# The four weight sums of the first z1 group, recorded seven z2 groups earlier on GpSimd

## The chip, the cores and the metric

The kernel runs on one core of one Trainium2 chip. The metric is the device time of one execution in microseconds; the figure for a kernel is the median of its runs. A core has five engines with a queue in order each: TensorE (PE, with its weight loads shown as PEld), VectorE (DVE), ScalarE (ACT), GpSimd (POOL) and SyncE (SP), which issues DMAs.

## The reference

The input `x` has 2048 rows of 1024. A first block adds to it a memory-augmented attention over the normalised rows (32 heads, four segments of 512). The second block, a gated MLP, is the part that matters here; cut to its core it is

```python
z  = gelu(layernorm(h) @ w_in)              # w_in: 1024 x 3584
z1 = z[..., :1792]
z2 = layernorm(z[..., 1792:])
g  = einsum('ts,bsf->btf', w_sp, z2) + b_sp[None, :, None]
h2 = h + (z1 * g) @ w_out                   # w_sp: 2048 x 2048, w_out: 1792 x 1024
```

All inputs and the output are bf16.

## The kernel before

The program is written with a recorder: every call `pe.matmul(...)`, `pool.tensor_tensor(...)` and so on is appended to the list of its engine, with the waits that follow from the memory it reads and writes. Each engine then works through its own list in order. **The order in which calls are recorded is thus the order of each engine's queue**; every instruction is issued from one helper line (L210 in the profile), so the profile is read by tile names.

The stages that touch the change:

* **z2 groups.** `z2_group(k, tc)` computes 128 rows (`tc`, 0 to 15) by 448 columns (`k`, 0 to 3) of the second half of `z`: eight matmuls of 128x448, then a gelu on ACT into `z`. The list `todo` gives their order. After each group `z2_stats` records `bn_stats` on DVE (`zst`); when `k` is 3 it also records the aggregate on DVE (`zmv`), and two tiny instructions on POOL that turn the variance into a reciprocal deviation (`zrs`, an add and a power).
* **The `aux` table.** `at(q, f, ...)` puts a small job beside a z2 group: group `(k, tc)` runs the jobs of `q = 16 k + tc - 20`, after its matmuls and gelu and before its statistics. So q = 29 is group (3, 1) and q = 36 is group (3, 8). In this table stand the squares of the `w_sp` rows (ACT, `sj`), the scaling of the z1 weights to f16 (`wz_half`, DVE, q = 26 to 33, tile `wzh`; the first tile's two halves are q = 26 and 27), half-sized differences of the normalised rows (`hn_sum`, DVE, tile `ht`; q = 28, 30, 32 and 34 for the second half of the rows), a cast on POOL at q = 37 (`sqb`), and the four weight sums of the first z1 group (`sz_sum(0, k)`, POOL, tile `sz`).
* **z1 steps.** The first half of `z` is computed transposed by a seven-product scheme in the manner of Strassen. There are 14 groups `g`; each has seven steps `z1_step(g, k)` of four matmuls of 128x512 on PE. Step 1, 2 and 4 use weights `wzh` as they are; steps 5, 6, 7 and 3 use the sums 1, 2, 3 and 4 of the group's weights, which `sz_sum` forms on POOL, one TENSOR_TENSOR of 128x512 f16 each. Sum 2 is made from sum 1, and sum 4 from sum 2. Sums 1 to 3 have one buffer each, shared by all groups; sum 4 has two in turn. The sums of group `g + 1` are recorded inside the steps of group `g`: sums 1 and 2 with step 5, sum 3 with step 7; sum 4 comes two groups ahead. For the first group there is no earlier one, so its sums stand in `aux`. Sum 4 of group 1 is recorded with step 2 of group 0.
* **Order of steps.** `offs = {1: -5, 6: 0, 5: 1, 7: 3, 2: 4, 4: 6, 3: 12}` is added to `7 g` and sorted. The first steps are therefore (0,1), (0,6), (0,5), (1,1), (0,7), (0,2), (0,4), (1,6), (1,5), (2,1), (1,7), where (g,k) is group and step. Later groups have one more step, (g-1,3), between (g,2) and (g,4).
* During z1 the scaled `z2h` is written too: on DVE (with step 6) and on ACT (with step 4, after a small POOL instruction `znm`).

After z1 come two gate stages with the product by `w_sp` (again seven products per group) and the product by `w_out`; the change touches none of them.

Of the kernel before, what the change touches and what calls it, by code (L numbers as in the profile page):

```python
# [258 lines left out]
def bass_sequential_preLN__memory_aug_infini_attn__mixer_gmlp__prompt_kernel(  # L259
# [734 lines left out]
    def at(q, f, *a):  # L994
        aux.setdefault(q, []).append((f, a))
# [18 lines left out]
    for k in range(4):  # L1014
        at(28 + 2 * k, hn_sum, 1, 1 + k // 2, k % 2)
    for k in (1, 2, 3, 4):
        at(35 + k, sz_sum, 0, k)

    todo = [(0, 2), (0, 3), (0, 8), (0, 9), 0, (0, 10), 1, (0, 11), 2, (1, 0), 3]
    todo += [(1, tc) for tc in range(1, 4)] + [(0, tc) for tc in range(12, NTC)]  # L1020
# [513 lines left out]
```

## Time and profile before

| | before |
|---|---|
| runs, us | 754.74, 755.83, 756.22 |
| median, us | 755.83 |
| profiled execution: span, us | 753.7 |
| profiled execution: own time beside the span | not given apart from the span |
| PE busy | 748.3 us (99%), 5470 matmuls |
| DVE busy | 557.1 us (74%) |
| ACT busy | 421.6 us (56%) |
| POOL busy | 296.3 us (39%) |
| chain that ended last | PE 90%, DMA 3%, ACT 3%, DVE 2%, POOL 2% |

The span runs from the first to the last instruction of one execution; times in the trace are counted from its start. In a timeline, a line is a start, a length and what ran, with the number of like instructions merged into it (x4); a bracket tells the idle time before it and what ended it. Matmuls overlap, so the length of a merged block is longer than the distance to the next one. The z2 groups of `k` = 3 lie at about 380 to 404 us, the z1 steps from 404.74 us on.

### The profile page before, as it was taken

The numbers are of one execution on the slowest core, as the hardware profiler recorded it, in microseconds if no ns is written. First come the engines' busy times: TensorE is split into PE (matmuls) and PEld (weight loads), VectorE is DVE, ScalarE is ACT, GpSimd is POOL, SyncE is SP. The second block draws the span as 40 slices with busy tenths as digits, with TensorE's granted clock in tenths as the row PEclk, the third lists the DMA queues.
The fourth block names the chain that finished last, engine by engine and source line by source line (L and its number), as shares of the span: only waits on it lengthen the run. The fifth ranks groups of instructions, "written<-read, shape, count | busy, mean of one in ns | idle before, by whom it ended". The sixth has DMA issues, their size and how long they took to land.

```text
span 753.7 us, 13510 instructions
## 1 busy us (share of the span) xinstructions
PE 748.3 (99%) x5470; PEld 359.1 (48%) x5470; DVE 557.1 (74%) x1013; ACT 421.6 (56%) x519; POOL 296.3 (39%) x450
## 2 busy tenths in 40 slices
PE   9999999999999999999999999999999999999998
PEld 4445455555554445545554444444444444444444
DVE  5585589768975576677986796997885385989776
ACT  6777877787777767325894879733231355300000
POOL 2565456555654334010039988622220011222342
PEclk9999999999999999999999999999999999999999
DMA  9554546444523331678650027330019961001211
GB/s 304 171 164 83 96 75 134 99 72 93 120 58 84 119 79 43 162 188 254 192 169 0 1 41 142 56 98 1 0 21 142 262 198 35 0 1 41 79 50 57
DMA packets 136783, 75.09 MB, mean 100 GB/s; under 512 B 98064, under 2 KB 126480, under 8 KB 136720
## 3 DMA queue, kind: packets, MB, share of 16 engines
q1 hardware_dynamic: 129184, 67.14, 37.0%
q10 hardware_dynamic: 7536, 7.08, 3.5%
q8 instruction: 43, 0.70, 0.4%
q14 instruction: 20, 0.16, 0.1%
HBM read 42.74 MB, written 8.39 MB: 68 GB/s over the span
## 4 chain that ended last, share of the span: by engine, by line
PE 90%; DMA 3%; ACT 3%; DVE 2%; POOL 2%; issue 0%; ACTq 0%; DVEq 0%
PE ps L210 90%; DMA sj<-in_B_w_sp_dram 2%; ACT sj L210 2%; POOL zrs L210 1%; DMA wv<-in_A_wv_dram 1%; POOL sz L210 1%; DVE zst L210 1%; ACT z L210 1%; DVE wzh L210 1%; DVE ht L210 0%; DVE zmv L210 0%; ACT L210 0%; DVE fin L210 0%; ACTq L210 0%; DVE top L210 0%
## 5 line engine op out<-in xcount | busy, mean ns | idle before, releaser
L210 ACT ACTIVATE e<-ps 128x2048 bf16<-128x2048 f32 (+1 forms) x96 | 152.6, 1590 | 41.7 <-PE ps L210 41.5
L210 POOL TENSOR_SCALAR_AFFINE_SELECT e<-e 128x512 bf16<-128x512 bf16 x128 | 90.9, 723 | 131.2 <-ACT e L210 131.2
L210 PE MATMUL ps<-win,hnT 128*128 128x448 bf16 x512 | 98.4, 352 | 0.0
L210 POOL TENSOR_TENSOR tmp_s1b<-tmp_s,brow 128x512 f32<-128x512 f32 x28 | 36.4, 1301 | 121.6 <-DVE tmp_u L210 63.0
L210 PEld LDWEIGHTS ps<-win,hnT 128*128 128x128 bf16 x512 | 49.6, 98 | 46.3 <-issue 0.2
L210 PE MATMUL ps<-xnT,wk 128*128 128x512 bf16 x256 | 60.8, 380 | 0.0
L210 DVE TENSOR_TENSOR zt<-ps,zt 128x512 f32<-128x512 f32 x70 | 48.2, 689 | 16.8 <-PE ps L210 13.5
L210 PE MATMUL ps<-xnT,wq 128*128 128x512 bf16 x256 | 60.5, 379 | 0.0
L210 PE MATMUL ps<-wv,xnT 128*128 128x512 bf16 x256 | 60.0, 381 | 0.3 <-DMA wv<-in_A_wv_dram 0.2
L210 PE MATMUL ps<-wo,oT 128*128 128x512 bf16 x256 | 58.0, 379 | 0.0
L210 ACT ACTIVATE z<-ps 128x448 bf16<-128x448 f32 x60 | 30.4, 545 | 33.4 <-PE ps L210 33.4
L210 PE MATMUL ps<-w_out,z1T 128*128 128x512 bf16 x224 | 48.6, 379 | 0.0
L210 DVE BATCH_NORM_STATS2 zst<-z 128x6 f32<-128x448 bf16 x64 | 37.9, 611 | 10.3 <-ACT z L210 10.2
L210 PEld LDWEIGHTS ps<-v,e 128*128 128x128 bf16 x1280 | 38.8, 96 | 14.0 <-issue 6.5
L210 DVE RECIPROCAL rd<-ps 128x16 f32<-128x16 f32 x32 | 8.0, 250 | 47.0 <-PE ps L210 46.8
L210 PE MATMUL ps<-v,e 128*128 128x33 bf16 x1280 | 42.2, 178 | 0.0
L210 ACT ACTIVATE tmp_s<-ps,invy 128x512 f32<-128x512 f32 x7 | 4.8, 688 | 63.3 <-POOL tmp_s1b L210 35.9
L210 POOL TENSOR_TENSOR sz<-wzh 128x512 f16<-128x512 f16 x28 | 34.5, 1232 | 8.3 <-PE ps L210 8.3
L210 PEld LDWEIGHTS ps<-wo,oT 128*128 128x128 bf16 x256 | 24.1, 98 | 27.5
L210 PEld LDWEIGHTS ps<-xnT,wk 128*128 128x128 bf16 x256 | 22.6, 98 | 29.9 <-issue 5.0
L210 ACT ACTIVATE z1T<-zt,inv 128x512 bf16<-128x512 f32 x42 | 29.0, 715 | 13.1 <-DVE zt L210 13.1
L210 PEld LDWEIGHTS ps<-wv,xnT 128*128 128x128 bf16 x256 | 23.1, 98 | 27.3 <-DMA wv<-in_A_wv_dram 0.9
(204 smaller groups left out, 1459.8 us busy)
## 6 DMA issues: line engine op xcount, KB each, us to landing
sj<-in_B_w_sp_dram SPq DMA_DIRECT2D x16, 512.0 KB, 3.7
xch<-in_A_x_dram SPq DMA_DIRECT2D x16, 256.0 KB, 3.7
xr<-in_A_x_dram SPq DMA_DIRECT2D x16, 256.0 KB, 4.0
out_dram<-hch SPq DMA_DIRECT2D x16, 256.0 KB, 2.4
win<-in_B_w_in_dram SPq DMA_DIRECT2D x4, 896.0 KB, 5.3
wz<-in_B_w_in_dram SPq DMA_DIRECT2D x6, 512.0 KB, 8.0
wo<-in_A_wo_dram SPq DMA_DIRECT2D x1, 2048.0 KB, 8.4
fin<-out_dram ACTq DMA_DIRECT2D x16, 128.0 KB, 3.1
```

The lines of the kernel that those rows point to most:

```text
L210: ins = getattr(e, op.name)(*op.args, **op.kw)
```

## The change

One number: the four sums of the first z1 group move from q = 36 to 39, z2 groups (3, 8) to (3, 11), to q = 29 to 32, groups (3, 1) to (3, 4). The instructions stay the same. In POOL's list each of them now stands ahead of seven `zrs` pairs that it stood behind; at q = 29 its jobs in `aux` stand behind the `wz_half` of that q, which is on another engine.

```diff
     for k in range(4):
         at(28 + 2 * k, hn_sum, 1, 1 + k // 2, k % 2)
     for k in (1, 2, 3, 4):
-        at(35 + k, sz_sum, 0, k)
+        at(28 + k, sz_sum, 0, k)
```

## The prediction, on record before the result

> **What bounds the kernel now.** I read the page first: TensorE (PE) is busy 748.3 of the 753.7 us, and 90% of the chain that ended last is PE work at a granted clock of 9 tenths or more in every slice. A change on another engine can therefore give only what PE spends waiting for that engine. So next came the waits, for 380 to 430 us, around the seam between the z2 groups and the z1 steps.
>
> ```profile
> PEld ps L210 <- POOL sz L210: 1.5, 1, 1.5
> PE ps L210 <- POOL sz L210: 1.0, 1, 1.0
> ```
>
> Columns: who waited for whom, total us, times, longest. GpSimd (POOL), writing a weight sum `sz`, holds PE up once; over the whole span PE's other waits are 1.2 and 0.2 us long and lie at the start. The PE timeline (start, length, instructions) shows where:
>
> ```profile
> 409.05 1.03 PE L210 MATMUL ps<-hnT,wzh 128*128 128x512 bf16 x4
> 410.00 1.04 PE L210 MATMUL ps<-z1x,wzh 128*128 128x512 f16 x4
> 412.06 1.90 PE L210 MATMUL ps<-z1x,sz 128*128 128x512 f16 x8 [1.02 <-POOL sz L210]
> ...
> 416.42 1.03 PE L210 MATMUL ps<-hnT,sz 128*128 128x512 bf16 x4
> 417.28 1.03 PE L210 MATMUL ps<-z1x,wzh 128*128 128x512 f16 x4
> ```
>
> Ends overlap, so I count starts. Undisturbed, a block of four takes 0.86 us (416.42 to 417.28). The block of 410.00 is step (0,4) of the first z1 group; the next, step (1,6), is due at 410.86 and starts at 412.06: **1.20 us lost**. It reads sum 2 of group 1. The chain in order of time says why that sum is late:
>
> ```profile
> 395.70 0.23 POOL zrs L210
> ...
> 397.40 1.12 POOL sz L210
> ...
> 403.41 1.12 POOL sz L210
> ...
> 409.64 1.13 POOL sz L210
> 410.78 0.07 issue
> 410.85 1.17 POOL sz L210
> 412.02 0.05 issue
> 412.06 338.53 PE ps L210 x1578
> ```
>
> From 395.70 to 412.02 the chain is POOL without a gap: the small `zrs` pairs of the z2 row statistics, the four sums of group 0 (the first at 397.40, the last at 403.41), more `zrs`, then sums 1 and 2 of group 1. POOL is a queue in order, and it runs behind. After 412.06 the chain is PE alone for 338.53 us.
>
> **The change, step by step.** Nothing is added or removed: four POOL TENSOR_TENSOR of 128x512 f16 (1.15 us each in their rows at 397 to 404) move ahead of seven `zrs` pairs each, the last three also ahead of a `sqb` CAST of 0.2 us. No DMA moves, and no queue but POOL's changes. The question is only whether POOL had room earlier.
>
> ```profile
> 374.31 0.20 POOL L210 CAST sqb<-sqz 128x14 bf16<-128x14 f32 x1 [43.37 <-DVE sqz L210]
> 387.93 0.58 POOL L210 TENSOR_SCALAR zrs<-zmv 128x1 f32<-128x1 f32 x1 [13.42 <-DVE zmv L210]
> 388.60 0.87 POOL L210 TENSOR_TENSOR zrs<-zrs,mhz 128x1 f32<-128x1 f32 x1
> 389.96 0.58 POOL L210 TENSOR_SCALAR zrs<-zmv 128x1 f32<-128x1 f32 x1 [0.50 <-DVE zmv L210]
> ```
>
> It had: 13.42 us idle before 387.93, then gaps of 0.50, 0.20, 0.50, 0.20 and 0.19 (1.59 us) up to 395.70.
> 1. The first sum needs the two halves of the first scaled weight tile; the second half, a VectorE (DVE) `wzh` of 0.73 us at 383.29, ends at 384.02. In the new order this sum stands ahead of the `zrs` pair of 387.93, so it runs at about 384.1 to 385.3, wholly in idle time: POOL's backlog loses 1.15.
> 2. The other three follow the first three `zrs` pairs and fill the 1.59 us of gaps. The last `zrs`, which ends now where the next sum starts (409.61), ends at 409.61 - 1.15 - 1.59 = 406.87 by POOL's work. Its input, the last `zmv` of DVE (406.17 + 0.26 = 406.43), allows 406.43 + 0.82 (a pair, 408.79 to 409.61) = 407.25. The later one holds: 407.25.
> 3. Sum 1 of group 1 overwrites what PE reads in the pair of blocks from 405.60 to 407.49. In later groups the sum follows such a pair by 0.09 us, so it can start at 407.58. **The backlog is no longer last; PE's own read is.**
> 4. Sums 1 and 2 together take 2.40 us now (409.61 to 412.01) and 3.01 where DVE works beside them (432.21 to 435.22). So sum 2 is seen by PE, 0.05 later, at 410.03 to 410.64. The weight load that needs it is due 0.21 us ahead of its matmul (417.93 for 418.14), at 410.65. Both ends are in time: the wait goes whole.
>
> What is late next: at (0,4) the load waits 0.41 for DVE, which still reads the bank; that follows PE and stays (0.09 by starts, so the gain is at most 1.29). Sum 1 of group 2 is freed by PE and has a full period of 6.05 us, as later groups, which show no such wait. Sums 3 and 4 of group 1 are read by the steps at 413.45 and later and are ready at about 411.1 and 412.2. Nothing behind 412 us waits on a clock of its own by the PE waits, so 1.20 should reach the end.
>
> **What could cost.** The sums move beside other DVE work. These rows, DVE and then POOL, bound it:
>
> ```profile
> 385.14 0.68 DVE L210 TENSOR_TENSOR ht<-hnT,hnT 128x1024 f16<-128x1024 bf16 x1
> ...
> 398.42 0.57 DVE L210 BATCH_NORM_STATS2 zst<-z 128x6 f32<-128x448 bf16 x1
> ...
> 432.55 1.64 DVE L210 TENSOR_TENSOR ht<-hnT 128x1024 f16<-128x1024 bf16 x1
> ```
>
> ```profile
> 432.21 1.44 POOL L210 TENSOR_TENSOR sz<-wzh 128x512 f16<-128x512 f16 x1 [0.88 <-PE ps L210]
> 433.73 1.49 POOL L210 TENSOR_TENSOR sz<-sz,wzh 128x512 f16<-128x512 f16 x1
> ```
>
> Beside statistics a sum takes 1.15 and disturbs nothing (0.57 at 398.42). Beside an `ht` subtraction both suffer: DVE 1.64 for 0.68 (+0.96), POOL 1.49 for 1.15 (+0.34). The new place has four `ht` (385.14 to 394.16) and DVE busy 7.53 of 7.70 us from 388.0. Low end: nothing. High end, POOL: three sums at +0.34 make 406.87 into 407.89, sum 2 is seen at 410.34 to 410.95, and up to 0.30 of the wait stays. High end, DVE: four times 0.96 is 3.84; DVE idles 2.01 of the 9.00 us from 395.70 and another 0.89 before 406.73, so its last `zmv` is 0.94 late, sum 2 is seen 0.62 later than in step 4, at 410.65 to 411.26, and up to 0.61 stays. PE itself reads none of this DVE work before 404.7. I take the low end, because the sums fall at about 384.1, 389.5, 392.0 and 394.4 (each pair and sum taking 2.5), where at most three can meet an `ht`: 2.88 of DVE delay, just inside its 2.01 + 0.89 = 2.90 of slack. The gain is 1.20, bounds 0.59 to 1.29.
>
> [...]
>
> **The sum.** The page gives no time of its own for the profiled execution beside the span of 753.7; the three runs (754.74 to 756.22) lie 1.0 to 2.5 above it, the median 2.13. 753.7 - 1.20 = 752.5 of span, and 752.5 + 2.13 = **754.63 us**, 0.16% less. What a measurement of this kernel can tell from no change is about 0.2%, 1.51 us, so I forecast a true gain that is just under that line.
>
> **Rivals.**
> - *Part of the wait stays* (bounds above): gain 0.59 to 0.9, 754.9 to 755.2. For it: the `ht` rows. Against: DVE's idle time after 395.70.
> - *Nothing changes*, because sum 2 is held by PE's read of its buffer and not by the backlog: 755.8. Against: sum 2's buffer is last read by the step of 405.60, long before 410.85, and POOL has no idle time before it.
> - *The wait is longer outside the profile.* If the runs stall as the load row says (1.51) or more, 754.3 or below. The profile can't exclude it.
> - *Slower: DVE is blocked for a whole sum each time.* Place: 384 to 396 us. Price: four times 1.49 = 5.96 of DVE delay, less 2.90 of slack: the last `zmv` comes 3.06 later, at 409.49, its `zrs` ends at 410.31, and sum 2 at 412.71 to 413.32 instead of 412.01. That is 0.7 to 1.3 slower, 756.5 to 757.1; it turns into a loss from a DVE delay of 4.7 to 5.3. Against: no row shows more than 0.96, and the statistics, half of DVE's work there, show none.
>
> **Chances.** Forecast 0.66, part stays 0.12, longer wait 0.10, no effect 0.07, slower 0.05. The runs before lie 1.48 apart, so a comparison may read 0.7 to either side; 1.51 is 0.31 from the forecast, and I give four in ten of its cases to "faster". Faster by over 0.2%: 0.4 x 0.66 + 0.10 + 0.02 = 0.38. Slower by over 0.2%: less than the slower rival's 0.05, as its price is mostly below 1.51: 0.04 with scatter. Within: 0.58. The range takes the forecast with 1.0 below it, and reaches above to the no-effect case with 0.4 of scatter: 753.6 to 756.2. It leaves out most of the slower rival.
>
> **What would show it.** Right: in the profile after, the first sum runs near 384.1 in what was idle time; POOL waits for DVE or PE again before 409; sum 1 of group 1 starts near 407.6; no PE wait for `sz` remains; blocks at 410.00 and 410.86; PE's chain from the seam to the end is as long as before. Wrong: a PE wait for `sz` or for DVE near 410, `ht` rows of 1.64 at 385 to 395 that push the last `zmv` beyond 406.6, or a new PE wait later that takes the 1.20 back.

## The result, and the profile after

| | before | after |
|---|---|---|
| median of 19 runs, us | 755.64 | 754.43 |
| lowest to highest, us | 754.74 to 756.22 | 753.47 to 755.12 |
| span of the profiled execution, us | 753.7 | 752.2 |
| chain that ended last | PE 90% | PE 98% |

The ratio is 0.9983, 95% interval 0.9977 to 0.9990: 1.21 us, where 1.20 was forecast. Measured again on another chip (11 runs) the changed kernel had 754.55 against 755.53, ratio 0.9988, interval 0.9979 to 0.9997. The gain is small; both intervals lie below 1, and both hold the forecast ratio of 0.9984 (754.63 to 755.83).

The PE timeline of the kernel after, at the seam (start, length, instructions):

```profile
409.65 1.04 PE L210 MATMUL ps<-z1x,wzh 128*128 128x512 f16 x4
410.56 1.90 PE L210 MATMUL ps<-z1x,sz 128*128 128x512 f16 x8
```

From step (0,4) to step (1,6) it is now 0.91 us instead of 2.06: 1.15 of the 1.20 are gone and 0.05 is left. The view of the waits still has one line for it, at the weight load, and PE's own row for `sz` has gone:

```profile
PEld ps L210 <- POOL sz L210: 0.4, 1, 0.4
```

The end of the chain in order of time: PE is on it without a break from 8.79 us to the last matmul. Before, the chain was on a DMA, ACT, DVE and POOL from 347.17 us to the seam.

```profile
8.79 740.31 PE ps L210 x5431
749.10 0.02 issue
```

The spans differ by 1.5, not 1.2, because in this execution the first z1 block also starts 0.35 us sooner (404.39 for 404.74). That belongs to the head of the program: there the chain waits for a first weight piece (`wv`), which lands at 8.74 us for 9.09. From step (1,6) to the end of PE's chain it is 338.54 us after (749.10 - 410.56) and 338.53 before: nothing is given back later.

POOL's timeline after, the bracket being idle time and what ended it:

```profile
383.73 1.15 POOL L210 TENSOR_TENSOR sz<-wzh 128x512 f16<-128x512 f16 x1 [8.55 <-DVE wzh L210]
388.14 0.59 POOL L210 TENSOR_SCALAR zrs<-zmv 128x1 f32<-128x1 f32 x1 [3.26 <-DVE zmv L210]
...
394.49 1.15 POOL L210 TENSOR_TENSOR sz<-wzh,sz 128x512 f16<-128x512 f16 x1
...
407.12 1.04 POOL L210 TENSOR_TENSOR zrs<-zrs,mhz 128x1 f32<-128x1 f32 x1
408.13 1.15 POOL L210 TENSOR_TENSOR sz<-wzh 128x512 f16<-128x512 f16 x1
409.36 1.15 POOL L210 TENSOR_TENSOR sz<-sz,wzh 128x512 f16<-128x512 f16 x1
```

The four sums run from 383.73 to 395.6. Sum 1 of group 1 starts at 408.13 instead of 409.61. It follows its `zrs` without a gap, about 1.0 us after PE's read of its buffer has ended (405.25 + 1.89 = 407.14). So in this execution POOL's queue still comes last, though PE loses only 0.05 us by it. The last `zrs` takes 1.04 us, where the ones just before it take 0.57; it runs beside DVE's scaling `z2h` (407.00 to 407.74).

What the move cost stands on DVE:

```profile
384.10 1.34 DVE L210 TENSOR_SCALAR wzh<-wz,sc 128x2048 f16<-128x2048 bf16 x1
385.35 0.68 DVE L210 TENSOR_TENSOR ht<-hnT,hnT 128x1024 f16<-128x1024 bf16 x1
...
390.00 1.34 DVE L210 TENSOR_SCALAR wzh<-wz,sc 128x2048 f16<-128x2048 bf16 x1
...
392.10 1.39 DVE L210 TENSOR_SCALAR wzh<-wz,sc 128x1024 f16<-128x1024 bf16 x1
...
394.83 1.08 DVE L210 TENSOR_SCALAR wzh<-wz,sc 128x1024 f16<-128x1024 bf16 x1
```

Four weight scalings beside the sums take 1.34, 1.34, 1.39 and 1.08 us where they took 0.73, 0.68, 0.42 and 0.42: 2.90 us more. The second and the third of them before:

```profile
389.79 0.68 DVE L210 TENSOR_SCALAR wzh<-wz,sc 128x2048 f16<-128x2048 bf16 x1
...
391.22 0.42 DVE L210 TENSOR_SCALAR wzh<-wz,sc 128x1024 f16<-128x1024 bf16 x1
```

The `ht` subtractions keep their 0.6 to 0.7. The stretch from 395.7 on shows what paid for it, before and then after (columns: stretch, length, then busy time of PE, PEld, DVE, ACT, POOL):

```profile
395.70:404.70 9.00, 9.00 (x49) 4.66 (x48) 6.99 (x18) 4.89 (x9) 8.58 (x16) 1.00 0.00 0
395.70:404.70 9.00, 9.00 (x49) 4.68 (x48) 8.66 (x23) 4.62 (x10) 7.76 (x21) 1.00 0.00 0
```

DVE had 2.01 us idle there and has 0.34.

### The profile page after: what moved, and what is told of

It reads as the page before. It is cut to its first block, busy times and chain, and to the rows that moved or that the text cites. A ratio compares the mean times of both kernels' runs of the same rounds, so it can differ in the third digit from the quotient of the medians.

```text
span 752.2 us, 13510 instructions
## 1 busy us (share of the span) xinstructions
PE 747.5 (99%) x5470; PEld 358.8 (48%) x5470; DVE 559.3 (74%) x1013; ACT 421.3 (56%) x519; POOL 297.0 (39%) x450
## 4 chain that ended last, share of the span: by engine, by line
PE 98%; DMA 1%; ACT 0%; DVE 0%; ACTq 0%; DVEq 0%; issue 0%
PE ps L210 98%; DMA wv<-in_A_wv_dram 1%; ACT L210 0%; DVE fin L210 0%; ACTq L210 0%; DVEq L220 0%; ACT rdm L210 0%
```

## The experiments

**Theory.** PE waits at step (1,6) because POOL's queue in order brings sum 1 and then sum 2 of group 1 too late; what helps is whatever shortens that queue. ("Queue" below is the time from POOL's first `zrs` to the start of sum 1 of group 1, and "the step" the time from the start of step (0,4) to the start of step (1,6), 0.86 us when nothing waits.) **Rivals.** (a) It matters that the sums of group 0 are formed early, not how long the queue is. (b) VectorE sets the pace of the seam, through the statistics. (c) The wait is something fixed.

**1. The queue refilled.** The changed kernel, with work put back on POOL that nobody waits for:

```diff
     for k in (1, 2, 3, 4):
         at(28 + k, sz_sum, 0, k)
+        at(35 + k, sz_sum, 0, 4)
```

> The changed kernel with sum 4 of group 0 formed again at q = 36 to 39 (the same values, written four times more): POOL gets its 4 x 1.12 us of backlog back, while the sums that PE needs stay early. Backlog theory (PE waits for sum 2 of group 1 because POOL runs behind): sum 2, seen at 410.56 in the changed kernel, comes 4.5 us later less the 0.4 us that POOL idles after 395.7, so the wait at step (1,6) is about 4 us and the time 758 to 759 us, ratio to before 1.003 to 1.005. Rival (the early sums themselves matter, not the length of POOL's queue): no wait, ratio 0.998 as for the change.

Measured: 759.79 against 755.68, ratio 1.0057 (1.0045 to 1.0070). PE's blocks, and the end of its chain:

```profile
409.89 1.04 PE L210 MATMUL ps<-z1x,wzh 128*128 128x512 f16 x4
414.44 3.37 PE L210 MATMUL ps<-z1x,sz 128*128 128x512 f16 x8 [3.52 <-POOL sz L210]
```

```profile
414.44 339.99 PE ps L210 x1578
```

The step takes 4.55 us, 3.69 over the undisturbed 0.86: the theory's wait of about 4. Rival (a) falls: all sums of group 0 are as early as in the changed kernel. The time lies above the expected range, for a reason that was not foreseen. After the wait the eight matmuls take 3.37 us, where the same block takes 1.90 above, and the rest of the chain is 339.99 instead of 338.5 us, 1.5 us more. The same columns as above, the granted clock third from the end:

```profile
414.44:417.60 3.16, 3.16 (x8) 1.13 (x9) 1.24 (x2) 0.61 (x1) 2.43 (x3) 0.53 0.00 0
```

The runs say the same: all five have a mean granted clock of 0.997 or 0.998 over the whole execution, where 26 of the 27 runs of the kernel before have 1.00, and 0.002 of 757 us is 1.5 us.

**2. Half of the refill, and three quarters.** As above, for `k < 3` and for `k < 4`.

> The changed kernel with sum 4 of group 0 formed twice more, at q = 36 and 37. Backlog theory: 2 x 1.12 us less 0.4 us of POOL idle time, so PE's wait at step (1,6) is about 1.9 us, 0.7 us over that of before: ratio 1.0005 to 1.0015. A us of POOL work in the queue is a us of time.

Measured: 756.33 against 755.53, ratio 1.0009 (0.9999 to 1.0018). The step takes 3.41 us in the profile, a wait of 2.55, which is more than the 1.9 expected. The profiled execution is the slowest of its eleven (757.38); the medians, at the expected ratio, put the loss against the changed kernel on that chip at 1.78 us (756.33 - 754.55).

> The changed kernel with sum 4 of group 0 formed three times more, at q = 36 to 38, between the two earlier refills. Two gave a wait of 2.55 us at full TensorE clock and four gave 3.69 us, after which TensorE ran eight matmuls at a granted clock of 0.53. Expected: a wait of about 3 us (1.16 for each sum, moved by up to 0.6 us with how late VectorE is in that execution); if the clock drop needs the longer idle time, full clock and ratio 1.002 to 1.003; if a drop, 1.0 to 1.5 us more, ratio 1.004.

Measured: 758.94 against 755.76, ratio 1.0035 (1.0022 to 1.0048). The step takes 3.71, a wait of 2.85, and the clock stays at 1.00. The runs are of two kinds, 757.2 (two) and 758.9 to 759.5 (three); the profile is of the first kind. The runs' own clocks tell the kinds apart: 1.00 in the two, 0.998 in the three, the same 1.5 us as in experiment 1. How long PE waited in those three no profile shows.

**3. The sums stay late but leave POOL.** The kernel before, with

```diff
-    def sz_sum(g, k):
+    def sz_sum(g, k, eng=pool):
...
-        pool.tensor_tensor(sz(g, k), a, b, op)
+        eng.tensor_tensor(sz(g, k), a, b, op)
...
-        at(35 + k, sz_sum, 0, k)
+        at(35 + k, sz_sum, 0, k, dve)
```

> The kernel before, its four sums of group 0 still at q = 36 to 39 but on DVE. Backlog theory: POOL loses 4.5 us of queue, the z2 statistics' last input from DVE (406.4) becomes last, sum 2 of group 1 is in time or at most 0.3 us late, gain 0.9 to 1.2 us, ratio 0.9983 to 0.9989, though nothing is formed earlier. DVE has 2.0 us idle there and pays about 4 x 0.35 us. Rival (the sums have to be early): ratio 1.000.

Measured: 754.47 against 755.68, ratio 0.9985 (0.9975 to 0.9996), the whole gain without forming anything sooner. The seam, on PE and on POOL:

```profile
410.13 1.04 PE L210 MATMUL ps<-z1x,wzh 128*128 128x512 f16 x4
411.00 1.89 PE L210 MATMUL ps<-z1x,sz 128*128 128x512 f16 x8
```

```profile
407.70 1.52 POOL L210 TENSOR_TENSOR sz<-wzh 128x512 f16<-128x512 f16 x1 [0.19 <-PE ps L210]
```

No wait is left (0.87 us), and sum 1 of group 1 now waits for PE, not for the queue: the bracket of 0.19 is what step 3 of the prediction had expected of the change itself. The four sums take 0.36 to 0.39 us each on DVE.

**4. Only the first sum moved**, the other three as before:

```diff
-        at(35 + k, sz_sum, 0, k)
+        at(29 if k == 1 else 35 + k, sz_sum, 0, k)
```

> The kernel before with only the first of the four sums moved, to q = 29; the other three stay at q = 37 to 39. Backlog theory: this sum alone leaves the backlog, 1.12 us, as it runs before POOL's first row statistics; the wait of 1.20 us shrinks to 0.1 to 0.4 us, gain 0.8 to 1.1 us, ratio 0.9985 to 0.9990. If the gaps between the first statistics had to be filled as well, the gain would be under half of 1.2 us, ratio 0.9993 or more.

Measured: 754.79 against 755.68, ratio 0.9990 (0.9982 to 0.9999), which is as expected. Its profile is not: the step takes 1.75 us, a wait of 0.89 where 0.1 to 0.4 was expected. That execution was the slowest of eleven (755.61), so it was profiled again.

> The kernel of the third experiment, profiled once more, since the execution profiled there was the slowest of its runs. If the wait at step (1,6) is the time at which sum 1 of group 1 starts, counted from the first z1 block, less 3.67 us, it is so here too; POOL's queue is 20.8 us long again (20.76 there), and the wait is 0.9 us where VectorE is as late as there and down to 0.1 us where it is 0.8 us earlier.

Measured: queue 20.87 us, step 1.21 (410.67 to 411.88), wait 0.35; one time, 755.21. Moving the first sum alone brings part of the gain; by how much the wait shrinks, 0.31 to 0.85, differs from one execution to the next. In the second POOL's queue starts 16.85 us ahead of the first z1 block, in the first 16.20.

**5. All four at q = 28**, in POOL's idle time before its first statistics:

```diff
-        at(35 + k, sz_sum, 0, k)
+        at(28, sz_sum, 0, k)
```

> All four sums of group 0 at q = 28, one after the other in the 4.4 us in which POOL idles before its first row statistics. Backlog theory: POOL is no longer behind at all, the 0.05 us of wait that the changed kernel keeps at step (1,6) goes too, gain 1.2 us, ratio 0.9983, the same as the changed kernel within 0.1%. Rival (VectorE blocked by the sums makes the last z2 statistics late): four sums in a row beside the weight scalings cost VectorE 2 us or more, its last aggregate comes after 407, and 0.5 us or more of the wait is back, ratio 0.999 or more.

Measured: 754.37 against 755.68, ratio 0.9985 (0.9976 to 0.9994). The wait is gone to the last hundredth (0.87 from 409.98 to 410.85). Rival (b) does not come true. VectorE does lose time, on two kinds of instruction:

```profile
384.54 1.33 DVE L210 TENSOR_SCALAR wzh<-wz,sc 128x2048 f16<-128x2048 bf16 x1
385.80 1.64 DVE L210 TENSOR_TENSOR ht<-hnT,hnT 128x1024 f16<-128x1024 bf16 x1
...
387.89 1.11 DVE L210 TENSOR_SCALAR wzh<-wz,sc 128x2048 f16<-128x2048 bf16 x1
```

Those three cost 0.60, 0.96 and 0.38 us more than in the kernel before, and a fourth 0.13; the last three sums take 1.48, 1.60 and 1.60 us for 1.15. DVE's idle time covers its part: its last `zmv` starts at 406.15, no later than before (406.17). This is as fast as the changed kernel and not faster, as 0.05 us was all there was to gain.

**6. The cover taken away.** Six more statistics on DVE, repeats into the same place, once in the kernel before and once in the changed one:

```diff
+    for k in range(6):
+        at(35 + k, dve.bn_stats, ZST[:, 0, 2, :], Z2[:, 0, 896:1344])
```

> The kernel before with six more VectorE statistics of 0.55 us (3.3 us, each a repeat of an earlier one into the same place) at q = 35 to 40. Theory: VectorE has 2.9 us idle between 395.7 and 406.7, so its last aggregate comes 0.4 us later at most, and POOL, which is behind, doesn't reach it before 408.8 anyway: no change, ratio 1.000 within 0.0005. Rival (VectorE already paces the seam): 3 us more, ratio 1.004.

Measured: 755.91 against 755.53, ratio 1.0010 (1.0001 to 1.0019). The wait in the profile is 1.12 us and the span 753.6, as before (1.20 and 753.7). The runs are 0.4 us slower, twice what was expected at most in ratio, and this profile does not explain it: its execution (755.30) is the second fastest of the eleven.

> The changed kernel with the same six VectorE statistics (3.3 us) at q = 35 to 40. Theory: the moved sums have used up VectorE's idle time (0.34 us left of the 9 us from 395.7), so the last aggregate, ended at 406.09, comes about 2.9 us later, the last row statistic of POOL ends near 409.8, sum 2 of group 1 comes near 412.2, and PE waits 1.5 us or more: the gain is gone, ratio 0.9995 to 1.001. Rival (the slack is still there): ratio 0.998.

Measured: 756.70 against 755.53, ratio 1.0018 (1.0009 to 1.0026). The gain is gone and more; the loss was underrated. PE's blocks show two waits, and the first is not POOL's:

```profile
407.91 1.03 PE L210 MATMUL ps<-hnT,wzh 128*128 128x512 bf16 x4
410.20 1.04 PE L210 MATMUL ps<-z1x,sz 128*128 128x512 f16 x4 [1.26 <-DVE zt L210]
...
412.03 1.04 PE L210 MATMUL ps<-z1x,wzh 128*128 128x512 f16 x4
413.63 1.90 PE L210 MATMUL ps<-z1x,sz 128*128 128x512 f16 x8 [0.57 <-POOL sz L210]
```

DVE is so late with its statistics that its first `zt`, which reads out `ps`, holds up step (0,7): 2.29 us, 1.43 too many. Then POOL, whose last statistics come late too, adds 0.74. Together that is 2.17, which is 0.97 more than the wait before; 1.17 was measured. The same 3.3 us cost 0.4 us before the change and 2.15 (756.70 - 754.55, on one chip) after it. The moved sums have spent DVE's cover.

**7. Three groups sooner** instead of seven:

```diff
-        at(35 + k, sz_sum, 0, k)
+        at(32 + k, sz_sum, 0, k)
```

> The kernel before with the four sums three groups sooner, at q = 33 to 36. If POOL's backlog starts only where its row statistics no longer wait for VectorE, these sums fill just the two last gaps (0.20 and 0.19 us) and meet no weight scaling but the last: the wait at step (1,6) shrinks from 1.20 to 0.8 to 1.0 us, ratio 0.9994 to 0.9998. Rival (any earlier place gives the gain in proportion to its distance, 3 of 7): wait 0.7, ratio 0.9993. Rival (all of the gain, as the first sum no longer stands in the dense part): ratio 0.9984.

Measured: 755.25 against 755.76, ratio 0.9994 (0.9985 to 1.0003). The time lies in the expected range, where the interval also holds no gain at all; the profile has a wait of 0.34, less than expected. It does not tell the theory from its rivals.

**8. The kernel before, profiled again.**

> The kernel before, profiled once more. POOL's queue is 21.7 us long again and the wait follows its start by the same rule: 1.2 us where the queue starts 16.8 us before the first z1 block, less by as much as it starts earlier, and more if it starts later. Rival (the wait is a fixed 1.20 us): 1.20 whatever the start.

Measured: queue 22.05 us, start 17.19 us ahead of the first z1 block (16.81 in the first profile), wait 1.19. The queue started 0.38 sooner, was 0.37 longer, and the wait stayed, as the rival has it: a wait of 0.8 was expected. So half of the rule falls, that the wait follows the start of the queue: the queue has no fixed length. The 0.37 are not waits for DVE; those come to 1.62 us here and 1.59 in the first profile. They fall on a `zrs`, 0.21 us long just before and after, which runs beside DVE's `z2h` by estimate: that starts 2.60 us after the first z1 block in the first profile (407.34 - 404.74) and 2.61 in the changed kernel's, which makes it 407.82 to 408.56 here:

```profile
407.94 0.69 POOL L210 TENSOR_SCALAR zrs<-zmv 128x1 f32<-128x1 f32 x1
```

The repeat of the changed kernel, last:

> The changed kernel again, on the chip of the three others: 0.998.

Its times stand with the result above. In its profile the step is 0.88 us (410.45 to 411.33), and sum 1 of group 1 starts at 408.02, 2.83 us after the first z1 block (405.19), where the first profile of that kernel has 3.74:

```profile
408.02 1.52 POOL L210 TENSOR_TENSOR sz<-wzh 128x512 f16<-128x512 f16 x1
```

**All profiles together.** The other half of the rule, that the wait follows the start of sum 1, holds in every profile in which PE waits for sum 2. Let S be the start of sum 1 of group 1, counted from the first z1 block (0,1). In the kernel before S = 409.61 - 404.74 = 4.87, and the wait is 1.20; so S - 3.67 should be the wait (in the first row it is so by construction).

| kernel | S | S - 3.67 | wait measured |
|---|---|---|---|
| before | 4.87 | 1.20 | 1.20 |
| before, again | 4.86 | 1.19 | 1.19 |
| before + 6 on DVE | 4.79 | 1.12 | 1.12 |
| first sum only; again | 4.56; 4.02 | 0.89; 0.35 | 0.89; 0.35 |
| three groups sooner | 4.01 | 0.34 | 0.34 |
| after | 3.74 | 0.07 | 0.05 |
| after + 2 sums | 6.24 | 2.57 | 2.55 |
| after + 3 sums | 6.55 | 2.88 | 2.85 |
| after + 4 sums | 7.38 | 3.71 | 3.69 |
| after + 6 on DVE | 5.87 | 2.20 | 2.17, in two parts |

(In two of them one matmul of the first block is missing from the records; its start is taken as 0.86 before the next block.) Where S is below 3.67 there is next to no wait: S is 2.83 in the repeat of the changed kernel and with the sums on DVE, and 2.84 with all four at q = 28, and the waits are 0.02, 0.01 and 0.01. With two, three and four refilled sums the queue is 22.06, 22.77 and 24.39 us long, against 19.99 and 19.54 in the two profiles of the changed kernel: roughly 1 us for each sum. PE's wait is POOL's lateness, to 0.03 us, and it is not fixed (rival (c)): it runs from 0.01 to 3.69.

## Why the prediction was right, step by step

* **The wait of 1.20 us is what can be gained**: right. 1.15 in the profile, 1.21 in the medians (0.98 on the second chip), and nothing given back behind it.
* **Step 1, the first sum in idle time**: right in place (383.73 for "about 384.1"). Not free: the `wzh` beside it takes 1.34 for 0.73, and POOL's first `zrs` waits for DVE's work behind that `wzh`.
* **Step 2, POOL's work ends 2.74 us sooner (1.15 + 1.59)**: mis-sized in the first profile. Against the first z1 block, sum 1 came 1.13 sooner (4.87 to 3.74). In these two profiles the difference is made up of three things (and 0.03 by which a sum holds the queue for 1.12, not 1.15): 0.40 us of the gaps remain; the statistics and casts take 16.23 us instead of 15.61 (19.99 us of queue less 0.40 and three sums of 1.12, against 21.68 less 1.59 and four); and the queue starts 0.56 later against PE, as its first input does, which is about what the `wzh` beside the first sum lost (0.60). 0.40 + 0.62 + 0.56 = 1.58, and 2.74 - 1.58 = 1.16. In the repeat DVE is 0.45 earlier against PE and the last `zrs` takes 0.57 for 1.04: there sum 1 came 2.04 sooner, where step 3 puts it (407.58 - 404.74 = 2.84 after the first z1 block; 2.83 measured).
* **Step 3, "the backlog is no longer last; PE's own read is"**: wrong for the first profile, where sum 1 starts 1.0 us after PE's pair of blocks ends. In the repeat it starts 0.08 after that end (406.05 + 1.89 = 407.94) and right behind the last `zrs`: the two come at the same time to 0.1 us. With the sums on DVE and with all four at q = 28 the step is plainly true; there the bracket names PE. So it depends on the execution which of the two is last.
* **Step 4, both sums are in time**: nearly, and with luck in the first profile. There PE sees sum 2 at 410.56, 6.17 us after the first z1 block, where the early end of this step has 5.29: 0.88 later. Of that, 0.62 is the room that the step leaves up to the load's due time, 0.21 the load's lead over its matmul, which cost nothing, and 0.05 the wait. The room was not put there for the error of steps 2 and 3.
* **What could cost**: the size was right by accident. The price was put on the `ht` subtractions, "at most three": 2.88 us. It fell on four `wzh` scalings, 2.90, and on no `ht`. The slack of 2.90 was read too large, as 0.30 of it (406.43 to 406.73) lies behind the last `zmv`; that `zmv` still starts 1.44 us after the first z1 block, for 1.43 before. DVE's idle time took the loss (2.01 us of it before and 0.34 after in the 9.00 us from 395.70).
* **Rivals**: "part stays" came to 0.05 and 0.02. "Nothing changes" is refuted by the result and by the refills. "The wait is longer outside the profile" isn't borne out: three profiles with the old order, one with extra DVE work, show 1.12 to 1.20, and the medians gained 1.21 and 0.98. A single execution can be longer: one of the 27 runs of the kernel before on one chip took 758.94 at a clock of 0.998, and no profile shows where. The slower rival, DVE blocked until PE waits, needed 4.7 us of DVE delay and got 2.9; with 3.3 of added statistics a loss of its size does come (1.17). Its way was incomplete: DVE's own `zt` stops PE before the late statistics do.

## What to carry to other kernels

A short wait of the bounding engine is worth its start-to-start excess (1.20 us here, where the medians gained 1.21 and 0.98), and a move on another engine's queue is worth how much sooner the awaited instruction starts there, not the sum of the instructions that left its way: the rest of the queue stretched here, from 15.61 to 16.23 us. One profile does not give that figure: two of the same kernel lay 0.91 us apart in it. Before work is moved beside another engine, look at which rows there could run longer beside it, all of them (here the `wzh` scalings, 1.08 to 1.39 us for 0.42 to 0.73), and at the idle time behind them; that idle time is what pays. And ask what is late next when it is spent: the changed kernel is faster and has less room than the one before.

## What the runs showed of the hardware that was not expected

* After PE had waited 3.52 us, its next eight matmuls ran at a granted clock of 0.53, which cost 1.5 us more; from 417.60 us on it was 1.00 again. Waits of 2.68 and 2.38 us in the profiles of the three and two refilled sums were followed by a clock of 1.00. No run here shows the length at which the clock falls.
* Beside a GpSimd sum a weight scaling on VectorE (bf16 to f16) took 1.08 and 1.39 us with 1024 elements (0.42 before) and 1.34 us with 2048 (0.73 and 0.68 before), in the first profile of the changed kernel. Its row ends 0.3 us (1024) or 0.5 to 0.6 us (2048) after the sum's row; why, no run shows. Statistics (`zst`) beside a sum keep their 0.6 us (0.63 and 0.57 at 397.58 and 399.99 in the kernel before).
* In the ten profiles read there on both engines an instruction that POOL has beside DVE's first `z2h` scaling takes longer: a `zrs` 1.04 us for 0.57 (after) or 0.68 for 0.22 (after + 4 sums), sum 1 itself 1.52 for 1.15 (after, again). Which one it is differs from one profile to the next; the queues of the two profiles of the changed kernel differ by 0.45 us, and the last `zrs` by 0.47.
